# Recurrent attention followed by a squared-ReLU layer: the loads of the last twelve chunks move from SyncE's queue to GpSimd's

## The chip, the core and the metric

The kernel runs on one core of one Trainium2 chip, as a single launch. The metric is the time of one execution on the device in microseconds (us). The profile is one execution recorded by the hardware profiler; its times count from the first instruction of the program.

## What is computed

The first stage is a gated linear recurrence over 768 tokens, for 4 batches of 8 heads with 48 numbers each. The second is a layer with 2048 hidden units that works on the 3072 tokens and needs the eight heads of a token side by side:

```python
for t in range(S):
    state = alpha[:, :, t, :, None] * state + einsum('bhd,bhe->bhde', k[:, :, t], v[:, :, t])
    y[:, :, t] = einsum('bhd,bhde->bhe', q[:, :, t], state)
x = y.transpose(0, 2, 1, 3).reshape(B * S, H * D)     # 3072 x 384
h = x @ w_in                                          # 384 -> 2048
g = relu(h) ** 2
out = g @ w_out                                       # 2048 -> 384
```

All inputs and the output are float32 in HBM. In q, k, v and alpha the head stands ahead of the token, so one token of one head is a run of 48 numbers, 192 bytes.

## The kernel before

**Tiles.** The 3072 tokens are cut into 24 chunks of 128, six per batch, numbered 0 to 23 (`s` in the code). A chunk of q, k, v or alpha is loaded as one tile of 128 tokens by 8 heads by 48 numbers: 192 KB, that is 1024 runs of 192 bytes on the HBM side. Each of the four tile names (`qt`, `kt`, `vt`, `at`) has six buffers (`LB = 6`), so the tile of chunk s can be loaded once the user of chunk s-6 is through. Chunks 0 to 3 have their alpha loaded jointly; from chunk 10 on, the alpha of a chunk is loaded together with q, k and v of the chunk before it.

**One chunk of the recurrence.** ScalarE (ACT) takes the logarithm of alpha into `L_s` (L396). TensorE (PE) sums it along the tokens with a triangular matrix; ACT takes the exponential with both signs (L451, L454, L462, L466). q is multiplied by the decay and k by its inverse on VectorE (DVE). PE forms the scores `sc` (L555), DVE masks them into `sm` (L561), PE multiplies by v and adds the share of the running state (`py`, L592 and L601), ACT casts the result into `xn` (L610), and it is turned into `xT_big`, the input of the layer. The state is updated by PE, DVE and ACT (L572, L581, L586).

From chunk 11 on (`RAW = 11`) q and k are not turned by PE. GpSimd (POOL) casts the loaded tiles to bfloat16 (`rawb`, L413), and a DMA transpose on SyncE's (SP's) queue turns them (`rawt`, L416); DVE multiplies the turned tiles by the turned decay (L507, L510). v is cast by POOL in every chunk (`vb`, L405). For chunks 18 to 22 `xn` too is turned by a DMA transpose on SP (L620).

**The layer.** Groups of one, two or four token tiles run through w_in (L663), ReLU on ACT (L676), the square on DVE (L684), w_out (L732), an eviction (L756, L758) and a store. Ten of the stores, those of token tiles 8 to 17, are issued by POOL (L772), the others by SP.

**The order of the work.** The kernel writes its own schedule. Every piece of work is an `Op` with an engine, a planned duration, its dependences, a priority and a planned latency to its result (`lat`). `Plan.run` (L96) takes at each step the piece that can start first, smaller priority numbers ahead of larger ones, and fixes with that the order of the instructions of every engine. A gate lets a chunk of the recurrence start only 3.7 token tiles ahead of the layer's progress (L834 to L839). The loads on SP are a queue of their own in the plan, called DMA, taken strictly in the order in which they were added, each with 1.0 us of planned transfer (`LD1`) and 2.4 us to its landing. DMA transposes (`TR`) and stores by SP (`OUT`) are planned apart from it and occupy the same DMA time. A piece on another engine that has `moves` occupies DMA time as well. Planned dependences set the order alone; on the chip an instruction waits for the data and buffers that it needs and for the instructions ahead of it on its engine.

Of the kernel before, what the change touches and what calls it, by code (L numbers as in the profile page):

```python
# [54 lines left out]
def after(op, x=0.0):  # L55
    return (op, x)
# [85 lines left out]
def kernel(  # L142
# [10 lines left out]
    nc = tc.nc  # L153
# [40 lines left out]
        out=utri_f, in_=utri_f, compare_op=ALU.is_ge, fill=0.0,  # L194
# [10 lines left out]
    for c in range(JN):  # L205
        blk = slice(JP * c, JP * c + JP)
        nc.gpsimd.affine_select(
            out=tri4[blk, 0:JW], in_=tri4[blk, 0:JW], compare_op=ALU.is_ge, fill=0.0,
# [27 lines left out]
    def pin(ins):  # L236
        tc.keep_in_program_order(ins)
# [4 lines left out]
    def tr(*a):  # L242
        pin(nc.tensor.transpose(*a))  # L243
# [21 lines left out]
    def add(eng, dur, emit, *deps, **kw):  # L265
        return plan.add(Op(eng, dur, emit, deps, **kw))
# [41 lines left out]
    C = [dict() for _ in range(NT)]  # L308
    state = {}
    SRC = dict(srcs)  # L310
    EARLY = 4
    RAW = 11
    XTURN = (18, 23)
    TLD, TLAT, TLATE = 1.0, 4.0, 2.0
    NR = 3
# [48 lines left out]
    def add_load(s, nm):  # L364
        d = C[s]
        b, c = divmod(s, NCH)

        def ld():
            if nm not in d:
                d[nm] = loads.tile([P, H, D], FP32, name=nm)  # L370
            pin(nc.sync.dma_start(out=d[nm], in_=SRC[nm][b, c]))
        prev = C[s - LB].get("use_" + nm) if s >= LB else None
        d["ld_" + nm] = add("DMA", LD if s < 4 else LD1, ld, prev, lat=2.0 if s < 4 else LAG if s < 6 else 2.4, at=0.6)

    def add_chunk(s):
# [30 lines left out]

        raw = s >= RAW
        if raw:
            w, wz = s % NR, s % 2

            def e_rb(j, nm):
                raw_tiles()
                pin(nc.gpsimd.tensor_copy(R["b"][:, w, j, :, 0:D], d[nm]))  # L413

            def e_turn(j):
                pin(nc.sync.dma_start_transpose(out=R["t"][:, w, j], in_=R["b"][:, w, j].rearrange("p h d -> p (h d)")))  # L416
            rt = []
            for j, nm in enumerate(["qt", "kt"]):
                cb = add("POOL", 0.55, lambda j=j, nm=nm: e_rb(j, nm), d["ld_" + nm],
                         *([C[s - NR]["turn"][j]] if s >= RAW + NR else []), prio=-5.0)  # L420
                d["use_" + nm] = cb
                t_ = add("TR", TLD, lambda j=j: e_turn(j), cb, *([C[s - NR]["turned"][j]] if s >= RAW + NR else []), lat=TLAT)
                t_.late = TLATE
# [54 lines left out]
        if raw:  # L478
# [8 lines left out]
            aT = add("ACT", 0.48, e_AT, pT, after(ai) if ai else None, **g)  # L487
            aiT = add("ACT", 0.48, e_AiT, pT, after(aT), *([C[s - 2]["turned"][1]] if s >= RAW + 2 else []), **g)
            pT.gives = aiT
# [124 lines left out]
        def e_p4():  # L614
            d["px"] = psum(p4, [P, KT, P], BF16)
            for j in range(KT):
                tr(d["px"][:, j, :], d["xn"][:, j * P:(j + 1) * P], ident_bf)
        if XTURN[0] <= s < XTURN[1]:
            def e_xt():
                pin(nc.sync.dma_start_transpose(out=xT_big[:, :, s * P:(s + 1) * P], in_=d["xn"]))  # L620
# [164 lines left out]
    for d in DMA_ORDER + list(range(6, NT)):  # L785
        if d in ("i", "o"):
            load_w(d)
        elif d == "at":
            add_joint_alpha()
        elif isinstance(d, tuple):  # L790
            add_load(*d)
            if d[0] >= JN:
                if all("ld_" + nm in C[d[0]] for nm, _ in srcs):
                    add_chunk(d[0])
            elif d == JLAST:
                for s in range(JN):
                    add_chunk(s)
        else:
            for nm, _ in srcs:
                if nm != "at":  # L800
                    add_load(d, nm)
                elif d <= 9:
                    add_load(d, nm)
                if nm == "at" and 9 <= d < NT - 1:
                    add_load(d + 1, nm)
            add_chunk(d)
# [94 lines left out]
```

## Time and profile before

| what | value |
|---|---|
| median of 3 runs (lowest to highest) | 185.1 us (184.77 to 185.87) |
| the profiled execution's own time | 185.07 us |
| its span, first to last instruction | 183.4 us |
| TensorE clock granted | 1.00 throughout |
| PE / DVE / ACT / POOL busy in the span | 177.5 / 127.1 / 126.5 / 39.4 us |
| the four kinds of loads on SP, issue to landing, median | 3.6 to 4.0 us |
| ten stores on POOL, issue to landing, median | 3.1 us |

How to read it: an engine is busy while it executes; waits are not counted, nor is the issue of a DMA by SP. Of POOL, the busy time takes in the 5.5 us in which it issued its ten stores. One row of an issue shows how long it held its engine's sequencer, and another how long the data took to land. A "releaser" is what ended an engine's idle time. The DMA share is the mean busy share of the 16 DMA engines that serve all queues. In the rows of DMA queues, q1 is the hardware queue that SP feeds and q0 the software queue that POOL feeds.

### The profile page before, as it was taken

What the parts mean: (1) busy time and instruction counts of PE and PEld (TensorE: products, weight loads), DVE (VectorE), ACT (ScalarE), POOL (GpSimd) and SP (SyncE); (2) the same over time, 40 slices, a digit from 0 to 9 for tenths busy, and PEclk for the clock granted to TensorE, in tenths of its full rate; (3) what the DMA queues carried; (4) which work ended last, traced back from release to release, by engine and by line L of the source; (5) the groups of instructions that cost most, each with busy time, mean ns of one, the idle gap of its engine ahead of it and who ended that gap; (6) DMA issues with size and microseconds to landing.
All of it is one profiled execution on the core that took longest, in us unless ns stands there. A gap on an engine that the chain in (4) does not pass through costs nothing.

```text
span 183.4 us, 4946 instructions
## 1 busy us (share of the span) xinstructions
PE 177.5 (97%) x1908; PEld 130.5 (71%) x1908; DVE 127.1 (69%) x273; ACT 126.5 (69%) x286; POOL 39.4 (21%) x80
## 2 busy tenths in 40 slices
PE   7999999899999999999999998999999999999993
PEld 2577884567769877867768776667766777778663
DVE  1179898684999998778877867748855984744200
ACT  3677799226859996966967859847975895767321
POOL 8221100021131142132223133342323512000000
PEclk9999999999999999999999999999999999999999
DMA  5999999999999999998999599898898898901022
GB/s 168 215 212 252 302 366 321 326 220 204 177 191 201 194 179 173 141 190 161 150 193 202 113 240 186 161 227 162 170 201 182 176 163 194 301 13 43 12 77 86
DMA packets 120200, 34.12 MB, mean 186 GB/s; under 512 B 112400, under 2 KB 118928, under 8 KB 120176
## 3 DMA queue, kind: packets, MB, share of 16 engines
q1 hardware_dynamic: 119536, 31.83, 80.7%
q0 software_dynamic: 640, 1.97, 3.2%
q8 instruction: 15, 0.25, 0.6%
q14 instruction: 9, 0.07, 0.2%
HBM read 25.17 MB, written 4.72 MB: 163 GB/s over the span
## 4 chain that ended last, share of the span: by engine, by line
PE 49%; DMA 2%; ACT 1%; issue 0%; DVE 0%
PE bank L240 45%; DMA at<-in_alpha_dram 2%; PE sc L240 2%; PE st L240 1%; PE bank L243 1%; ACT aiT L454 0%; ACT r L676 0%; ACT ob L758 0%; ACT L_s L396 0%; ACT ob L716 0%; DVE xT_big L388 0%; ACT qkT L451 0%
## 5 line engine op out<-in xcount | busy, mean ns | idle before, releaser
L240 PE MATMUL bank<-xT_big,w_in_b 128*128 128x256 bf16 (+2 forms) x636 | 76.6, 262 | 0.9 <-ACT r L676 0.7
L240 PE MATMUL bank<-w_out_b,gT 128*128 128x384 bf16 (+1 forms) x400 | 71.6, 320 | 0.5 <-DVE w_out_b L296 0.5
L676 ACT ACTIVATE r<-bank 128x512 bf16<-128x512 f32 x96 | 56.6, 606 | 11.3 <-PE bank L240 9.9
L240 PEld LDWEIGHTS <-w_in_b 128*128 128x128 bf16 x636 | 52.7, 98 | 10.6 <-issue 1.5
L240 PEld LDWEIGHTS <-gT 128*128 128x128 bf16 x416 | 37.2, 98 | 18.7 <-DVE w_out_b L296 1.0
L684 DVE TENSOR_TENSOR gT<-r 128x512 bf16<-128x512 bf16 x96 | 41.8, 453 | 10.2 <-ACT r L676 9.0
L561 DVE TENSOR_TENSOR sm<-sc,utri_b 128x512 bf16<-128x512 f32 x48 | 30.8, 684 | 5.9 <-PE sc L240 5.7
L405 POOL CAST vb<-vt 128x384 bf16<-128x384 f32 x24 | 13.6, 569 | 69.1 <-DMA vt<-in_v_dram 55.2
L386 ACT CAST xn<-bank 128x384 bf16<-128x384 f32 x24 | 11.6, 482 | 11.6 <-PE bank L240 11.5
L505 DVE TENSOR_TENSOR kI_s<-kt,Ainv 128x384 bf16<-128x384 f32 x21 | 12.8, 611 | 7.8 <-ACT Ainv L466 7.8
L240 PEld LDWEIGHTS <-qkT 64*128 64x128 bf16 (+1 forms) x272 | 10.7, 95 | 6.4 <-issue 2.4
L586 ACT CAST sb<-st 128x384 bf16<-128x384 f32 x20 | 9.6, 482 | 7.7 <-DVE st L581 7.5
L758 ACT COPY ob<-bank 128x384 f32<-128x384 f32 x14 | 6.7, 480 | 8.0 <-PE bank L240 8.0
L396 ACT ACTIVATE L_s<-at 128x384 bf16<-128x384 f32 x20 | 10.5, 527 | 2.4 <-DMA at<-in_alpha_dram 2.3
L240 PE MATMUL bank<-warm 128*128 128x256 bf16 (+1 forms) x54 | 10.9, 348 | 1.3 <-DVE warm L188 1.3
L502 DVE TENSOR_TENSOR qA_s<-qt,A 128x384 bf16<-128x384 f32 x11 | 6.3, 575 | 8.0 <-ACT A L462 8.0
L413 POOL CAST rawb<-qt 128x384 bf16<-128x384 f32 x13 | 7.4, 570 | 20.3 <-DMA qt<-in_q_dram 20.3
L413 POOL CAST rawb<-kt 128x384 bf16<-128x384 f32 x13 | 7.6, 587 | 19.0 <-DMA kt<-in_k_dram 11.1
L581 DVE TENSOR_TENSOR st<-st,ae_s 128x384 f32<-128x384 f32 x20 | 11.1, 556 | 0.5 <-PE st L240 0.5
L466 ACT ACTIVATE Ainv<-bank 128x384 bf16<-128x384 f32 x21 | 10.5, 501 | 1.1 <-PE bank L240 1.0
L240 PE MATMUL sc<-qkT 64*128 64x128 bf16 x192 | 9.5, 219 | 0.0
L240 PEld LDWEIGHTS <-sm 128*128 128x128 bf16 x192 | 8.1, 96 | 1.7 <-issue 0.2
(64 smaller groups left out, 165.7 us busy)
## 6 DMA issues: line engine op xcount, KB each, us to landing
qt<-in_q_dram SPq DMA_DIRECT2D x24, 192.0 KB, 4.0
kt<-in_k_dram SPq DMA_DIRECT2D x24, 192.0 KB, 3.6
vt<-in_v_dram SPq DMA_DIRECT2D x24, 192.0 KB, 3.8
at<-in_alpha_dram SPq DMA_DIRECT2D x20, 192.0 KB, 4.0
wo<-in_moe_w_out_dram SPq DMA_DIRECT2D x4, 768.0 KB, 8.5
out_dram<-ob POOLq DMA_DIRECT2D x10, 192.0 KB, 3.1
wi<-in_moe_w_in_dram SPq DMA_DIRECT2D x4, 384.0 KB, 5.3
wi<-in_moe_w_in_dram SPq DMA_DIRECT2D x2, 768.0 KB, 8.3
```

What stands on the lines that cost most here:

```text
L240: pin(nc.tensor.matmul(*a, **kw))
L386: pin(nc.scalar.copy(out_t, in_t))
L396: pin(nc.scalar.activation(L[:, :, 0:D], d["at"], AF.Ln))
L405: pin(nc.gpsimd.tensor_copy(d["vb"], d["vt"]))
L413: pin(nc.gpsimd.tensor_copy(R["b"][:, w, j, :, 0:D], d[nm]))
L466: pin(nc.scalar.activation(d["Ai"], d["pm"][:, 0:HD].rearrange("p (h d) -> p h d", h=H), AF.Exp, scale=-1.0))
L505: pin(nc.vector.tensor_mul(kI[:, :, 0:D], d["kt"], d["Ai"]))
L561: pin(nc.vector.tensor_mul(d["sm"][:, hh], d["sc"][:, hh], utri_b.to_broadcast([P, NP, P])))
L581: pin(nc.vector.tensor_mul(st4, st4, bcast(ae, D)))
L586: pin(nc.scalar.copy(d["sbt"], d["st"]))
L676: pin(nc.scalar.activation(box["r"][:, 0:w], box["ph"][:, 0:w], AF.Relu))
L684: pin(nc.vector.tensor_mul(gT[g][:, f0:f0 + per, lo * P:lo * P + n], r, r))
```

## The change

Three constants are added, and a branch in `add_load`. For chunks 12 to 23 the tiles `at`, `qt`, `kt` and `vt`, 48 loads, are issued by POOL in place of SP. In the plan such a load takes 0.9 us of POOL, 0.85 us of DMA time and 5.0 us from the end of its issue to its landing; it may start once the scores (`p2`) of the chunk three before it are done, and its priority (4.0) stands behind that of the casts (-5.0) and ahead of that of POOL's stores (5.0). The size and the layout of each load, the buffers and everything that uses the tiles stay as they are. SP keeps its loads up to chunk 11, the weights, all DMA transposes and its stores. As the schedule is worked out anew, the order of the instructions can change on every engine.

```diff
@@ -310,6 +310,7 @@
     SRC = dict(srcs)
     EARLY = 4
     RAW = 11
+    PL, PL_AHEAD, PL_LAT = 12, 3, 5.0
     XTURN = (18, 23)
     TLD, TLAT, TLATE = 1.0, 4.0, 2.0
     NR = 3
@@ -368,8 +369,12 @@
         def ld():
             if nm not in d:
                 d[nm] = loads.tile([P, H, D], FP32, name=nm)
-            pin(nc.sync.dma_start(out=d[nm], in_=SRC[nm][b, c]))
+            pin((nc.gpsimd if s >= PL else nc.sync).dma_start(out=d[nm], in_=SRC[nm][b, c]))
         prev = C[s - LB].get("use_" + nm) if s >= LB else None
+        if s >= PL:
+            o = d["ld_" + nm] = add("POOL", 0.9, ld, prev, C[s - PL_AHEAD]["p2"], prio=4.0, lat=PL_LAT)
+            o.moves = 0.85
+            return
         d["ld_" + nm] = add("DMA", LD if s < 4 else LD1, ld, prev, lat=2.0 if s < 4 else LAG if s < 6 else 2.4, at=0.6)
 
     def add_chunk(s):
```

## The prediction

> **What bounds the kernel now.** I read the engines' totals first, then the table by stages, then the chain of work that ended last, then the rows of single operations that the change moves.
>
> ```profile
> PE 177.5 (97%) x1908; PEld 130.5 (71%) x1908; DVE 127.1 (69%) x273; ACT 126.5 (69%) x286; POOL 39.4 (21%) x80
> ```
> ```profile
> 60.00:80.00 20.00, 20.00 (x244) 16.19 (x241) 18.31 (x39) 16.60 (x39) 5.48 (x10) 1.00 0.96 174
> 80.00:100.00 20.00, 19.92 (x210) 14.79 (x209) 15.54 (x34) 14.98 (x35) 5.90 (x11) 1.00 1.00 176
> 100.00:120.00 20.00, 19.33 (x197) 14.24 (x196) 14.48 (x34) 15.84 (x37) 5.80 (x11) 1.00 0.90 180
> 120.00:140.00 20.00, 20.00 (x202) 14.09 (x199) 13.44 (x28) 14.52 (x35) 7.28 (x14) 1.00 0.91 189
> 140.00:160.00 20.00, 20.00 (x212) 15.18 (x211) 14.52 (x30) 14.75 (x34) 4.38 (x8) 1.00 0.88 200
> ```
>
> The columns are the stretch, its length, then PE, PEld, DVE, ACT and POOL busy, the clock, the DMA share and GB/s. The loads of chunks 12 to 23 lie between 60 and 150 us. There PE is idle for 0.08 + 0.67 = 0.75 us of 100. Its busy time is no stretched figure: in the chain below, 57 matmuls of the layer and the recurrence follow each other in 5.98 us, 105 ns apart. So PE's own work sets the time, and an earlier landing can give back 0.75 us at most. The chain has the one place where a load reached PE:
>
> ```profile
> 105.28 4.13 DMA at<-in_alpha_dram
> ...
> 109.42 0.34 ACT L_s L396
> ...
> 110.70 0.60 ACT aiT L454
> 111.30 0.49 ACT r L676
> 111.79 0.04 issue
> 111.84 0.49 PE bank L240 x3
> ...
> 146.09 5.98 PE bank L240 x57
> ```
>
> An alpha tile issued at 105.28 landed at 109.41. ACT, which works in order, stood at its logarithm; an eviction, two exponentials and a ReLU came late behind it, and PE waited 0.66 us for that ReLU. It is the whole loss of this stretch. After 162 us PE runs the rest of the layer, with no load left; before 60 us the loads are the same in both kernels.
>
> **The part taken from SP.** 48 of the 92 loads leave SP. While SP did little but load, 20 loads started from 39.98 to 60.76 us, 1.0 us apart, at a DMA share of 0.97. From 67 us on it has two transposes for each chunk besides. This frees SP and makes the transposes' issues earlier, by up to the load ahead of each, about 0.6 us; what they feed is hidden under PE's work, so I count 0. What is late next on SP is the POOL cast that a transpose needs.
>
> **The part put on POOL.** Each load's issue is a POOL instruction, in order with 36 casts and ten stores. The trace has POOL issuing stores alone, and SP issuing both kinds:
>
> ```profile
> L371 SPq DMA_DIRECT2D kt<-in_k_dram x24: 521/597/2482, 2.4 to 146.1; - x24
> L413 POOL CAST rawb<-kt x13: 507/508/804, 67.8 to 149.9; 128x384 bf16<-128x384 f32 x13
> ```
> ```profile
> L772 POOL DMA_DIRECT2D out_dram<-ob x10: 539/539/692, 97.1 to 152.9; - x10
> L772 SPq DMA_DIRECT2D out_dram<-ob x5: 332/332/350, 159.2 to 178.4; - x5
> ```
>
> The three numbers are least, median and most ns of one. A store is 192 KB in 128 runs of 1536 bytes, a load 192 KB in 1024 runs of 192 bytes. POOL's price for 1024 runs is the unknown of this change. One end: the number of runs does not matter, 0.54 us. The other: all of it grows with the runs, 8 x 0.54 = 4.3 us. The nearest row for the step from one form to the other is SP's: 332 ns becomes 521, a factor of 1.57. I take the same factor, 0.54 x 1.57 = **0.85 us**; it is an estimate, since another engine does the work. (The plan books 0.9.)
>
> Room on POOL: chunk 9's scores, after which chunk 12's loads may start, ran at 64.6 us; the last load on SP now starts at 146.7, so POOL should be through at about 148. In these 83.4 us POOL was busy for 26.6, stores included. That leaves 56.8 us for 48 issues, **1.18 us each**. At 0.85 they take 41 us, and POOL is 81% busy. So they fit, with 0.33 us to spare on each: cost on the path 0. Behind a burst of four issues (3.4 us) wait casts of q, k and v and the ten stores. The cover for that is the earlier start. Scores follow each other every 6.8 us (83.8 us for chunk 12, 158.6 for chunk 23, over 11), so three chunks are 20.4 us. Chunk 23's k is issued 12.5 us ahead of its scores now (146.1) and would be at about 20.4 - 3 x 0.85 = 18. For alpha it goes the other way: chunk 23's is issued 25.8 us ahead now (132.8), then about 20; its use is some 5 us ahead of the scores, which leaves 15 us. Each issue also waits for its buffer, last used by the chunk six before; that chunk is three chunks past when the issue comes, so I count no wait. If one waited, all casts would queue behind it.
>
> The Trainium skill has a rule on this price. The row: nine of ten POOL issues lie within 1 ns of 539, beside a DVE that is busy 13 to 18 of every 20 us, while casts go from 507 up to 804. The page "SBUF — State Buffer", section "Who interferes with whom", says that DVE instructions with two SBUF inputs shut out POOL instructions that read SBUF, and that DVE copies within SBUF in a two-port mode shut out even the writing of descriptors. By that rule, the trace agrees for the casts; whether a longer issue is hit more, no row here shows. By the row the sum stays; if the rule reached the issues too, it would be the waiting variant of rival (a).
>
> **DMA time.** A load on SP takes 1.0 us of all 16 engines (above). POOL's ten stores took 3.2% of 183.4 us for 1.97 MB, 0.59 us each:
>
> ```profile
> q1 hardware_dynamic: 119536, 31.83, 80.7%
> q0 software_dynamic: 640, 1.97, 3.2%
> ```
>
> The packet counts show why the two differ: q0 moved 3.1 KB per packet, q1 0.27 KB. A load on q0 lies between 0.59 (packed like the stores) and 1.0 us (no gain), or above if q0 reads short runs worse; nothing here excludes that, and twice SP's price is the bound I keep. I take 0.85. The four loads of a chunk then need 3.4 us in place of 4.0, at a share of 0.9 that is not the limit of PE: 0. At 2.0 us, four loads would need 8 us of every 6.8. Landing: the median is 3.1 us for POOL's stores, and 3.6 to 4.0 for loads on SP; the plan's 5.0 covers both.
>
> **The sum**, against the profiled execution (185.07 us, beside a median of 185.1): PE's work 0; the alpha wait gone, -0.66 at best; issues on POOL 0; a few new waits of a tenth of a us, as the order is planned anew, +0.2 to +0.5. That is -0.5 to +0.5; I take **184.9 us**.
>
> **Rivals.**
> (a) *POOL becomes the bound.* Above 1.18 us per issue every further 0.1 us costs 48 x 0.1 = 4.8 us, since casts, transposes, scores and then PE wait for POOL's order. At 1.5 us: 48 x 0.32 = +15, 200 us. At 4.3: +150, 335 us. For it: an eightfold number of runs, worked out by software, and the casts' stretching. Against it: SP's factor of 1.57. If each issue waited for one DVE instruction of 0.45 us (squares: 41.8 us for 96), 0.85 would become 1.30, and the time 191.
> (b) *Late landings reach PE.* Every engine works in order, so a load later than planned does again what the alpha did at 105 us, 0.66 us each time. Transposes and loads, now in two queues, contend for DMA engines that are 0.9 busy. One event in two chunks gives 6 x 0.66 = +4, 189 us. It decides once landings pass the planned 5.0 us; SP's alpha loads reached 8.8. Against it: 5 us more lead for k and v.
> (c) *More than 0.5% faster.* It needs 0.93 us, and the stretch holds 0.75. Only a new order of PE that also removes idle time elsewhere would do: 184.0.
> (d) *It does not load earlier.* The dependence on the scores stands in the plan alone, and alpha and q hardly move ahead. Then nothing changes: 185.1, within the forecast.
>
> **How the numbers follow.** Forecast with (d), within 0.5%: 0.50; (a) 0.24; (b) 0.18; (c) 0.08. A measurement of this kernel can tell about 0.5% (0.93 us) from no change. So faster 0.08, same 0.50, slower 0.42. The likeliest case's own range is 184.3 to 185.9. For 8 in 10 the range takes in (b) and (a) up to 1.5 us per issue; above that lies about 0.13, below 184.0 some 0.05: **184.0 to 200 us**.
>
> **What would show it.** POOL's issue row for the loads: 0.85 us right, over 1.18 wrong, and then POOL would be busy without gaps from 65 us on and PE would wait for the products with `rawt`. PE's idle time in 60 to 160 us: below 0.75 confirms the floor; several us, spread by chunk, with releasers at loads or turned tiles, is (b). q0's share: 48 loads at 0.85 us are 22% of the span; over 30% means that q0 reads short runs worse. The wait of ACT for alpha at 105 us should be gone. The forecast fails if the issue price is misjudged; that is its weakest step.

## The result and the profile after

| | before | after |
|---|---|---|
| median of 22 runs each (lowest to highest) | 185.06 us (183.6 to 188.54) | 186.52 us (184.66 to 188.41) |
| ratio after / before, 95% interval | | 1.0073 (1.0049 to 1.0097) |
| profiled execution: own time / span | 185.07 / 183.37 us | 186.2 / 184.05 us |
| the time outside the span | 1.70 us | 2.15 us |
| PE idle in 60 to 160 us | 0.75 us | 1.30 us |

The changed kernel is slower by 0.73%, about 1.4 us. The forecast was 184.9 us and no difference that can be told; the time lies in the range of 184.0 to 200, on the side that had the chance 0.42. Below, two profiled executions (of e9 and e12) took longer throughout than their kernels usually do, so only what lies behind their span and their fetches of instructions are read.

Lines of the code after `add_load` have moved down by 5: L421 is L416 of before, L625 is L620. First the engines' totals of the changed kernel:

```profile
PE 177.0 (96%) x1907; PEld 130.5 (71%) x1908; DVE 127.4 (69%) x274; ACT 126.2 (69%) x285; POOL 80.8 (44%) x128
```

POOL went from 39.4 to 80.8 us, the others stayed. The stages, with the columns of the prediction (stretch, length, PE, PEld, DVE, ACT, POOL, clock, DMA share, GB/s):

```profile
60.00:80.00 20.00, 19.87 (x242) 16.05 (x239) 18.10 (x40) 15.64 (x36) 14.19 (x20) 1.00 0.97 173
80.00:100.00 20.00, 19.99 (x213) 14.77 (x210) 15.03 (x32) 14.84 (x35) 16.50 (x24) 1.00 1.05 180
100.00:120.00 20.00, 19.76 (x202) 14.73 (x201) 16.63 (x36) 16.16 (x37) 15.39 (x23) 1.00 1.01 179
120.00:140.00 20.00, 20.00 (x204) 14.28 (x203) 13.41 (x28) 14.68 (x36) 17.11 (x25) 1.00 0.80 178
140.00:160.00 20.00, 19.08 (x201) 14.33 (x200) 12.96 (x27) 14.20 (x34) 6.25 (x11) 1.00 0.86 221
```

PE lost 0.24 us in 100 to 120, where it had lost 0.67, and 0.92 us in 140 to 160, where it had lost nothing. The chain that ended last shows what took the place of the alpha wait:

```profile
133.24 2.03 PE bank L240 x23
135.27 6.33 DMA xT_big<-xn
141.60 0.14 issue
141.74 4.17 PE bank L240 x36
```

PE's own sequence at that place, start and length first, shows the idle time in brackets:

```profile
140.46 0.36 PE L240 MATMUL bank<-vb,sm 128*128 128x48 bf16 x8
141.74 0.49 PE L240 MATMUL bank<-xT_big,w_in_b 128*128 128x256 bf16 x3 [0.92 <-DMA xT_big<-xn]
```

A transpose of `xn`, issued by SP at 135.27, landed at 141.60, 6.33 us later. The plan books 0.8 us for its issue and 4.0 us from there to its landing, 4.8 us in all. PE, in order, stood at the first product with that tile. No load was late: it is a transpose on SP's queue, which the change did not touch, that came late. How long the transfers took from issue to landing (kind, count, size, median us):

```profile
at<-in_alpha_dram POOLq DMA_DIRECT2D x12, 192.0 KB, 4.9
qt<-in_q_dram POOLq DMA_DIRECT2D x12, 192.0 KB, 5.1
kt<-in_k_dram POOLq DMA_DIRECT2D x12, 192.0 KB, 5.2
vt<-in_v_dram POOLq DMA_DIRECT2D x12, 192.0 KB, 4.6
...
rawt<-rawb SPq DMA_TRANSPOSE x26, 5.3
...
xT_big<-xn SPq DMA_TRANSPOSE x5, 3.3
```

Before, the same two rows of transposes stood at:

```profile
rawt<-rawb SPq DMA_TRANSPOSE x26, 3.4
...
xT_big<-xn SPq DMA_TRANSPOSE x5, 2.5
```

Last, the time outside the span. The DMA view of the 2.3 us behind the changed kernel's last instruction shows one packet; the same view of the kernel before shows none:

```profile
DMA packets 1, 0.01 MB, mean 4 GB/s; under 512 B 0, under 2 KB 0, under 8 KB 0
...
q14 instruction: 1, 0.01, 1.0%
```
```profile
DMA packets 0, 0.00 MB, mean 0 GB/s; under 512 B 0, under 2 KB 0, under 8 KB 0
```

It is a block of 8 KB of instructions, whose fetch begins 1.0 us after the last instruction of the span. The program's time is 0.45 us longer outside the span. This is not the mark of one execution: the changed kernel's 22 runs have 2.11 to 2.27 us outside the span, by the span that is listed for each, and all runs of the kernel before beside the experiments 1.66 to 1.84.

The accounting between the two profiled executions (+1.13 us) is then: +0.45 outside the span; +0.55 of PE's idle time in 60 to 160 us (1.30 against 0.75); +0.63 of idle time before 60 us, where both kernels load through SP alone; and -0.5 of PE's busy time (177.0 against 177.5). The last two are one execution against another: an unaltered second profile of the changed kernel (c1, below) has 5.3 us of idle time before 60 us where this one has 2.9.

### The profile page after: what moved, and what is told of

Same layout as the page of the kernel before. It is cut to its first block, busy times and chain, and to the rows that moved or that the text cites. A ratio compares the mean times of both kernels' runs of the same rounds, so it can differ in the third digit from the quotient of the medians.

```text
span 184.0 us, 4932 instructions
## 1 busy us (share of the span) xinstructions
PE 177.0 (96%) x1907; PEld 130.5 (71%) x1908; DVE 127.4 (69%) x274; ACT 126.2 (69%) x285; POOL 80.8 (44%) x128
## 4 chain that ended last, share of the span: by engine, by line
PE 70%; DMA 11%; DVE 9%; ACT 6%; issue 2%; SPq 0%; DVEq 0%; ACTq 0%
PE bank L240 62%; DMA wi<-in_moe_w_in_dram 5%; DVE gT L689 3%; DMA xT_big<-xn 3%; PE bank L243 3%; PE sc L240 3%; ACT r L681 2%; DMA at<-in_alpha_dram 2%; PE st L240 2%; DVE sm L566 1%; ACT A L467 1%; ACT Ainv L471 1%; DVE st L586 1%; DVE kI_s L510 1%; DVE w_out_b L296 1%
## 5 line engine op out<-in xcount | busy, mean ns | idle before, releaser
L240 PE MATMUL bank<-xT_big,w_in_b 128*128 128x256 bf16 (+2 forms) x635 | 75.5, 262 | 1.5 <-DMA xT_big<-xn 0.9
L689 DVE TENSOR_TENSOR gT<-r 128x512 bf16<-128x512 bf16 x96 | 42.8, 465 | 6.2 <-ACT r L681 5.3
L410 POOL CAST vb<-vt 128x384 bf16<-128x384 f32 x24 | 14.9, 622 | 53.9 <-DMA vt<-in_v_dram 49.2
L510 DVE TENSOR_TENSOR kI_s<-kt,Ainv 128x384 bf16<-128x384 f32 x21 | 12.2, 582 | 10.2 <-ACT Ainv L471 9.9
L240 PE MATMUL bank<-warm 128*128 128x256 bf16 (+1 forms) x54 | 10.0, 325 | 1.3 <-DVE warm L188 1.3
L372 POOL DMA_DIRECT2D at<-in_alpha_dram x12 | 10.8, 903 | 0.1
L372 POOL DMA_DIRECT2D qt<-in_q_dram x12 | 10.6, 885 | 0.0
L372 POOL DMA_DIRECT2D vt<-in_v_dram x12 | 10.6, 884 | 0.0
L372 POOL DMA_DIRECT2D kt<-in_k_dram x12 | 10.6, 883 | 0.0
```

Source lines behind the costliest of these rows:

```text
L240: pin(nc.tensor.matmul(*a, **kw))
L372: pin((nc.gpsimd if s >= PL else nc.sync).dma_start(out=d[nm], in_=SRC[nm][b, c]))
L410: pin(nc.gpsimd.tensor_copy(d["vb"], d["vt"]))
L510: pin(nc.vector.tensor_mul(kI[:, :, 0:D], d["kt"], d["Ai"]))
L689: pin(nc.vector.tensor_mul(gT[g][:, f0:f0 + per, lo * P:lo * P + n], r, r))
```

## The experiments

Three theories were at stake. **A, the queue:** POOL's loads make SP's transposes land later, and a late turned tile reaches PE. **B, the order:** the plan came out in another order, and that order costs something on whatever queue the loads are. **C, the code,** formed after the first four runs: the 0.45 us outside the span depend only on where POOL's program ends within a block of instructions. "Ratio" is against the kernel before, run on the same chip, with its 95% interval.

### e1: the new order, with all loads on SP

```diff
-            pin((nc.gpsimd if s >= PL else nc.sync).dma_start(out=d[nm], in_=SRC[nm][b, c]))
+            pin(nc.sync.dma_start(out=d[nm], in_=SRC[nm][b, c]))
```

> The changed kernel's plan and order of instructions, but the 48 loads are issued by SP in the places that the plan gives them. Theory A (what costs is the queue: turned tiles land late beside POOL's loads, and some 0.5 us that lie outside the span come with POOL's loads): the time outside the span goes back from 2.2 to 1.7 us, transposes land in about 3.4 us again, PE's wait for xT_big is gone, ratio to the kernel before 0.998 to 1.003. Theory B (the new order costs, whichever queue carries the loads): ratio 1.005 to 1.010 as in the change itself, with PE's wait for xT_big still there.

Measured: ratio 0.9998 (0.9956 to 1.0039). PE's idle time in 60 to 160 us is 0.24 us, and 1.71 us lie outside the span. `rawt` lands as early as before in the median, and the latest takes 4.8 us instead of 7.8 in the changed kernel; `xT_big` does not, 4.0 us against 2.5:

```profile
rawt<-rawb SPq DMA_TRANSPOSE x26, 3.4
...
xT_big<-xn SPq DMA_TRANSPOSE x5, 4.0
```

The median of five tiles tells little here; the tile that PE waited for, that of chunk 19, tells more. With the loads on SP it landed after 4.62 us, in time for PE; with the loads on POOL after 6.33, and after 5.86, 5.99 and 6.36 us in c1, e7 and e10 below; in e11, where SP loads again from chunk 18 on, after 3.57.

So the new order in itself costs nothing that can be measured, and the alpha wait goes in it too. What the changed kernel loses comes with the other queue or with what its use adds to the program.

### e2 and e3: no `xn` turned by DMA, with the loads on POOL and on SP

In both kernels:

```diff
-    XTURN = (18, 23)
+    XTURN = (18, 18)
```

> The changed kernel, but chunks 18 to 22 turn xn on PE as all other chunks do (XTURN empty), so that nothing of the layer's input passes a DMA transpose. PE gets 5 x 0.17 = 0.8 us more work. Theory A, if the late xT_big is the loss inside the span (0.9 us): it loses the 0.9 and pays 0.8, so the time is that of the change, ratio 1.005 to 1.009, and only about 0.5 us above the same edit on the kernel before (the run beside this one). Theory B: 1.35 us above that run, ratio 1.010 to 1.013.

> The kernel before with XTURN empty, as the partner of the run with the changed kernel. Both theories: 5 x 0.17 = 0.8 us more on PE and nothing else, ratio 1.003 to 1.006.

Measured: 1.0129 (1.0067 to 1.0191) with the loads on POOL, 1.0049 (1.0009 to 1.0088) on SP. The two are 0.8% apart. That is the number of theory B (1.010 to 1.013 and 1.35 us), not that of theory A (0.5 us), though the two intervals overlap; e1 speaks against B's reason, since there the same kind of new order cost nothing. PE's idle time in 60 to 160 us is 0.78 us on POOL and 0.00 on SP; `rawt` lands after 5.8 and 3.6 us. That suggests that `xT_big` is not the only tile through which the queue costs something. The time outside the span was 1.76 us in e2, though all 48 loads are on POOL: the 0.45 us are no price of POOL's loads. That led to theory C.

### e4: the loads on SP, and POOL's ten stores on SP too

```diff
-    POOL_OUT = (5, 18)
+    POOL_OUT = (5, 5)
```

> The kernel before with its ten stores on SP too, so that POOL issues no DMA at all. If the time outside the span grows with the number of DMAs issued by POOL (0.5 us for 48 loads, 0.01 each), it falls by only 0.1 us, from 1.7 to 1.6; if the first use of POOL's queue has a fixed price, it falls by more, and the 0.5 us of the change come from something else. The time itself: within 0.5% of the kernel before by theory A, as the stores are off the path; SP's queue gets 10 x 0.33 us more.

Measured: 1.0118 (1.0052 to 1.0184), a miss. 1.71 us lie outside the span, so POOL's stores have no part in that; but ten more issues on SP cost 1.2%. PE's waits in 60 to 160 us (us in total, times, longest):

```profile
PE bank L240 <- DMA xT_big<-xn: 1.3, 2, 1.0
PE sc L240 <- DVE qkT L510: 1.1, 1, 1.1
```

Both are turned tiles that came late, here because SP had no time to issue their transposes: `xT_big` landed 2.3 us after its issue in the median, but the first four of its five issues came 3.0 to 4.8 us after the tile was cast, where the kernel before has 2.3 to 3.1. In the kernel before, SP had little time to give away: added up from its trace, its issues fill 92% of 66 to 148 us, in the changed kernel 44%.

### e9: eight instructions on POOL that do nothing

```diff
     nc.gpsimd.memset(L4[:, :, :, D:], 0.0)
+    pad_t = consts.tile([P, 32], BF16)
+    for _ in range(8):
+        nc.gpsimd.memset(pad_t, 0.0)
```

> The changed kernel with eight small memsets more on POOL, issued before its first cast, where POOL idles. The changed kernel's trace has a fetch of 8 KB of instructions 1.0 us after the end of the span, and POOL has fetched after 69 recorded instructions and ends at 196, about 128 further on. Theory C (the 0.45 us outside the span are POOL's next block of instructions, asked for only at the program's end): with eight more instructions the fetch comes before the end, beside other work, and the time outside the span falls from 2.17 to 1.72 us, ratio to the kernel before 1.003 to 1.006. Rival (0.45 us is a price of POOL's loads as such, for their queue at the program's end): still 2.17 us, ratio 1.007.

Measured: 0.9997 (0.9954 to 1.0041). Outside the span lie 1.76 us, and the view of the stretch behind it has no packet:

```profile
DMA packets 0, 0.00 MB, mean 0 GB/s; under 512 B 0, under 2 KB 0, under 8 KB 0
```

The packet of 8 KB is now at 159.0 us, in the midst of the work. Eight more instructions took 0.39 us from the time outside the span, and in all 12 runs of e9 it lies between 1.67 and 1.81 us. The ratio came out below the forecast of 1.003 to 1.006, with an interval that takes in its lower end.

### e12: the kernel before, with 57 such instructions at the end of POOL's program

```diff
+    pad_t = consts.tile([P, 32], BF16)
...
+    for _ in range(57):
+        pin(nc.gpsimd.memset(pad_t, 0.0))
```

> The kernel before with 57 memsets of 32 numbers at the end of POOL's instructions, after its last store, where POOL only waits for the end: 139 + 57 = 196 recorded instructions, as many as in the changed kernel, and not one load moved. Theory C (POOL's next block of instructions is fetched at the program's end): the time outside the span rises from 1.72 to 2.17 us, the span stays, ratio 1.0025, with a fetch of 8 KB just after the span's end. Rival (the 0.45 us need loads issued by POOL): 1.72 us, ratio 1.000.

No load is moved here; POOL's program has only become as long as in the changed kernel (196 recorded instructions). Measured: 1.0024 (0.9975 to 1.0073), 2.19 us outside the span, and the packet is behind the span:

```profile
DMA packets 1, 0.01 MB, mean 3 GB/s; under 512 B 0, under 2 KB 0, under 8 KB 0
...
q14 instruction: 1, 0.01, 0.7%
```

With e9 this shows from both sides that the 0.45 us go with the length of POOL's program, and not with its loads: in all 12 runs of e12 2.12 to 2.21 us lie outside the span, in the 29 of the kernel before beside it 1.68 to 1.84. The ratios do not resolve it: 0.45 us are 0.24%, and each interval is wider. That a block is fetched behind the span is not enough, though: in e2 and e15 a fetch begins 0.6 us behind it, and only 1.76 and 1.78 us lie outside.

### e7 and e10: a realistic landing planned for the `xn` transposes

```diff
-            d["x"] = add("TR", 0.8, e_xt, xn, lat=TLAT)
+            d["x"] = add("TR", 0.8, e_xt, xn, lat=6.0)
```

e10 has the eight instructions of e9 as well.

> The changed kernel, but the plan books 6.0 us in place of 4.0 for the landing of the five turned xn, so that PE's order asks for them later. Theory A (inside the span the loss is PE's wait for a turned xn that landed 6.3 us after its issue): the wait of 0.9 us is gone, and nothing takes its place, ratio 1.001 to 1.004, with 2.1 to 2.2 us outside the span unless POOL's instruction count changes. Theory B (other small waits of the new order make the loss): ratio stays at 1.006 to 1.008, with waits at masks and turned tiles.

> Both edits at once, the eight memsets and the 6.0 us. Theories A and C together: both terms gone, ratio 0.998 to 1.001, and 1.72 us outside the span. If only one of the two holds, 1.002 to 1.005.

Measured: e7 1.0003 (0.997 to 1.0036), e10 1.0021 (0.998 to 1.0062). The wait for `xT_big` is gone in both, though the transposes land no earlier (4.4 us in the median). PE's idle time in 60 to 160 us is 0.74 and 0.56 us; e7 has 2.15 us outside the span, as theory C has it for an unpadded program, e10 1.84. e10 came out above its forecast of 0.998 to 1.001, which lies in its interval. That the two edits add up is not to be seen in the times.

### e11: POOL loads chunks 12 to 17 only

```diff
-            pin((nc.gpsimd if s >= PL else nc.sync).dma_start(out=d[nm], in_=SRC[nm][b, c]))
+            pin((nc.gpsimd if PL <= s < XTURN[0] else nc.sync).dma_start(out=d[nm], in_=SRC[nm][b, c]))
...
-        if s >= PL:
+        if PL <= s < XTURN[0]:
```

> POOL loads chunks 12 to 17 only; SP loads 18 to 23 again, as in the kernel before, so that no load is in POOL's queue while xn of chunks 18 to 22 is turned. Theory A (loads of the other queue delay the turned tiles): rawt of chunks 12 to 17 still lands late (5 us), xT_big lands in 2.5 us again and PE does not wait for it; POOL's instructions end away from a block's edge, so 1.72 us outside the span; ratio 0.998 to 1.002. Theory B: ratio 1.004 to 1.007, since most of the new order is kept.

Measured: 1.0013 (0.9978 to 1.0049), with no wait for `xT_big`. Its use is that one execution holds both queues. From 66 to 104 us POOL has most of the loads (21, beside 7 of SP), and the DMA view says:

```profile
q0 software_dynamic: 1338, 4.11, 55.5%
...
rawt<-rawb SPq DMA_TRANSPOSE x11, 6.1
```

From 110 to 150 us all loads are SP's:

```profile
q0 software_dynamic: 482, 1.45, 16.2%
...
rawt<-rawb SPq DMA_TRANSPOSE x11, 3.4
```

The same transposes, eleven in each stretch, land after 6.1 us beside POOL's loads and after 3.4 us beside SP's. The engines were somewhat busier in the first stretch too (q0 and q1 together 109% of their time, by the sum of the packets' times, against 94%); how much of the 2.7 us is due to that, e11 does not tell. The kernel before and the changed one tell something in 110 to 150 us, where q0 and q1 together take 88% of the engines' time in both: `rawt` lands there after 3.4 us in the one and 4.4 in the other. With e1 this shows the first half of theory A: `rawt` lands later where POOL loads. By what means is not shown.

### c1: the changed kernel once more, unaltered

> The changed kernel once more, unaltered, as a control beside the two others of this call. Expected again: ratio 1.005 to 1.010 and 2.17 us outside the span. If it comes out at 1.002 to 1.004, the share inside the span is smaller than the first measurement had it, and the time outside the span is most of what can be told apart.

Measured: 1.0036 (0.9995 to 1.0078), 2.15 us outside the span, and the wait at the same place of the chain, now 0.4 us long:

```profile
134.98 2.04 PE bank L240 x23
137.02 5.86 DMA xT_big<-xn
```

PE's idle time in 60 to 160 us is 0.70 us against 1.30 in the first profile. So the two marks, the late tile and the packet at the end, come back each time, and the size of the first varies.

### e13: the alpha wait of the kernel before mended in the plan

```diff
-        d["ld_" + nm] = add("DMA", LD if s < 4 else LD1, ld, prev, lat=2.0 if s < 4 else LAG if s < 6 else 2.4, at=0.6)
+        d["ld_" + nm] = add("DMA", LD if s < 4 else LD1, ld, prev, lat=2.0 if s < 4 else LAG if s < 6 else 4.2 if nm == "at" else 2.4, at=0.6)
```

> The kernel before with 4.2 us in place of 2.4 planned for the landing of the alpha loads from chunk 6 on, so that ACT's order asks for the logarithm when the tile is there. If the wait at 105 us is what an earlier alpha could give back (0.66 us), PE has no wait between 60 and 160 us, ratio 0.995 to 0.998. If other waits take its place, 0.999 to 1.004.

Measured: 1.0142 (1.0101 to 1.0182), a miss. The wait of 0.66 us is gone, a wait of 1.0 us behind an exponential (`ae_s`) came at about 62 us, and the time rose by 1.4%. A new order can cost more than the wait for which it was made; one wait taken off is no forecast of a time.

### e14 to e17: eleven `xn` turned by SP instead of five

Both kernels with chunks 12 to 22 turned by DMA, which takes 18 of 57 matmuls of `xn` off PE; without and with the planned landing of 6.0 us:

```diff
-    XTURN = (18, 23)
+    XTURN = (12, 23)
```

e14 is that edit in the kernel before, e15 in the changed one. e17 is e14 with the edit of e7, and e16 is e15 with those of e7 and e9.

> The kernel before, with xn turned by SP from chunk 12 on (eleven chunks in place of five). PE saves 6 x 0.17 = 1.0 us. Theory A: the turned xn share a queue with the loads and land in about 2.5 us, so no new wait, ratio 0.994 to 0.998, unless SP, which has four loads and two transposes for each chunk already, issues them late.

> The changed kernel, with xn turned by SP from chunk 12 on. PE saves the same 1.0 us. Theory A: the turned xn meet POOL's loads eleven times, land in 3 to 6 us against 4.0 planned, and PE waits for two or three of them, 1.5 to 3 us in all; ratio 1.005 to 1.015, and at least 1.5 us above the partner with loads on SP. Theory B (the order as such): PE's waits for xT_big do not grow, ratio 1.000 to 1.004.

> The same, with 6.0 us planned for the landing of the turned xn and the eight memsets on POOL that move its instruction block. Theory A: PE's waits for xT_big are gone, PE keeps the 1.0 us that it saves, ratio 0.994 to 0.999, which would be the fastest of the kernels with loads on POOL. Theory B: as in the run before this one, less 0.45 us at most.

> The kernel before with xn turned by SP from chunk 12 on and 6.0 us planned for its landing, as the partner of the run above with loads on SP. Both theories: 0.994 to 0.999; if SP is too full for eleven more transposes, waits for turned tiles appear and it comes out above 1.000, and the run with loads on POOL beats it.

| | loads on SP | loads on POOL |
|---|---|---|
| eleven `xn` turned by SP | e14: 1.0309 (1.0227 to 1.0391) | e15: 0.998 (0.994 to 1.002) |
| the same, landing of 6.0 us planned | e17: 1.0274 (1.0206 to 1.0342) | e16: **0.9865** (0.981 to 0.992) |
| PE idle in 60 to 160 us | 2.88 and 4.46 us | 0.81 and 0.00 us |

For e15 theory A wanted 1.005 to 1.015, as more tiles can be late: a miss. The waits for `xT_big` came to 0.2 us only. e14 (0.994 to 0.998 forecast) missed as well, and e16 gained more than its forecast of 0.994 to 0.999; e17 came out as its second case had it. On SP the same edit costs about 3%, and SP's own sequence in e17 suggests why (start, length, instruction):

```profile
118.83 1.20 SPq L416 DMA_TRANSPOSE rawt<-rawb  x1
120.08 0.58 SPq L371 DMA_DIRECT2D qt<-in_q_dram  x1
120.77 1.20 SPq L416 DMA_TRANSPOSE rawt<-rawb  x1
122.01 0.58 SPq L371 DMA_DIRECT2D kt<-in_k_dram  x1
122.64 0.58 SPq L371 DMA_DIRECT2D vt<-in_v_dram  x1
123.26 0.79 SPq L371 DMA_DIRECT2D at<-in_alpha_dram  x1
124.15 1.88 SPq L620 DMA_TRANSPOSE xT_big<-xn  x1
126.14 1.20 SPq L416 DMA_TRANSPOSE rawt<-rawb  x1
```

Each instruction begins within 0.11 us of the end of the one before. SP is full with its issues, and the chain of e17 runs through three of these issues and the landing of the v load after them:

```profile
120.08 0.58 SPq L371
...
120.77 1.20 SPq L416
...
122.01 0.58 SPq L371
...
122.64 3.75 DMA vt<-in_v_dram
```

With the loads on POOL these issues are gone from SP, and the plan with the longer landing keeps PE busy without a gap. How much of the distance between e16 and e17 is the order's, and not the queue's, was not tried: e16's order with its loads on SP is missing. The stage of 60 to 160 us in e16, then in e17:

```profile
60.00:160.00 100.00, 100.00 (x1073) 76.11 (x1068) 78.26 (x160) 78.66 (x182) 70.71 (x99) 1.00 0.99 192
```
```profile
60.00:160.00 100.00, 95.54 (x1014) 71.06 (x1012) 72.52 (x153) 73.48 (x172) 26.99 (x50) 1.00 0.99 181
```

e16 is the fastest kernel of the study, faster than both. Its profiled execution beats that of the changed kernel by 186.2 - 182.54 = 3.66 us: 1.9 of PE's busy time (177.0 to 175.1; the 18 matmuls are an estimated 1.0 of it, at 0.17 us for three, and the rest is not explained), 1.3 of PE's idle time over the whole span (7.0 to 5.7) and 0.44 outside the span.

## Why the prediction was wrong, point by point

**PE bounds the kernel, with 0.75 us to gain:** right. Nothing in the result asks for another bound; e16 gains 2.5 us on the profiled execution of before, and PE's busy time falls by 2.4 (177.5 to 175.1).

**POOL's issue price, 0.85 us, and its room:** right. The least, median and most ns of a k load and of a store on POOL:

```profile
L372 POOL DMA_DIRECT2D kt<-in_k_dram x12: 882/882/891, 69.2 to 140.0; - x12
```
```profile
L777 POOL DMA_DIRECT2D out_dram<-ob x10: 540/569/572, 96.3 to 153.6; - x10
```

0.88 us, 1.55 times the median store of this kernel and 1.64 times the 0.54 of the kernel before, where SP's factor of 1.57 had been taken. Some luck is in this: the factor came from SP's least issue of a load, 521 ns, and its median of 597 would have made it 1.80 and the price 0.97 us. In 64.6 to 148 us POOL was busy for 66.73 of 83.4 us, 80%, where 81% had been worked out. Rival (a) is out: PE's waits name no cast by POOL. Nor did the waiting variant come true: these twelve issues lie within 9 ns of each other. (In the prediction's row of stores it is eight of ten that lie at 539 ns; a ninth took 542.) By the rule of the Trainium skill ("SBUF — State Buffer", "Who interferes with whom") DVE copies within SBUF in a two-port mode would hold up the issues; between 66 and 142 us DVE's copies all read the matmul banks, so no run here tests that.

**DMA time of a load, 0.85 us:** too low, and without effect. The shares of the queues in the changed kernel:

```profile
q1 hardware_dynamic: 69616, 22.39, 53.3%
q0 software_dynamic: 3712, 11.41, 30.8%
```

q0 took 0.308 x 184.05 = 56.7 us, 5.9 of them for ten stores at 0.59; the rest over 48 loads is 1.06 us, against 1.0 on SP. All 48 take 27.6% of the span, where 22% had been worked out. q0 packs 16 runs into a packet (3072 packets for 48 loads, 3 KB each) and gains nothing by it.

**Landing within the planned 5.0 us:** right in the median (4.6 to 5.2 us from the start of the issue, where the plan has 0.9 and 5.0). No wait of PE or ACT names a load by POOL. Chunk 23's k was issued at 140.0, 18 us ahead of its scores at 158.0, as worked out. Its alpha was issued 20 us ahead, as worked out too, but its use was misread: the logarithm ran 11.8 us ahead of the scores and not 5, which left 8.3 us and not 15. That was enough.

**The alpha wait goes:** right. **Few new waits, +0.2 to +0.5 us:** this is the first step that failed. What the transposes feed was counted as "hidden under PE's work, so I count 0", with only the gain of an earlier issue in view, about 0.6 us. That gain was larger: SP issued the first four turned `xn` 2.3 to 3.1 us after their cast had ended in the kernel before, and at once (0.02 to 0.03 us) in the changed one. But the landing of the transposes went from 3.4 to 5.3 us for `rawt` and up to 6.3 for `xT_big`. Counted from the cast, four of the five `xT_big` still landed earlier than before; that of chunk 19 took 6.35 us instead of 5.10, PE asked for it 5.6 us after the cast, and so it reached PE (0.92 us, 0.4 in c1), with a wait of 0.24 us for a mask beside it. Late landings were named in rival (b), with contention of the two queues as the reason, which stays open; one came instead of six. In one execution it more than ate the 0.66 us of the alpha wait (idle 0.75 to 1.30), in the other it just balanced it (0.70).

**Time outside the span, unchanged:** this is the other step that failed. The sum was made against the profiled execution's own time, with what lies around the span taken as fixed. It rose by 0.45 us, as POOL's program had grown to a length at which another block of instructions is fetched behind the span (e9 and e12). It belongs to no rival.

**What stays open.** 0.45 us are a third of the loss of 1.4 us. The waits that the traces show inside the span explain between nothing and 0.6 us more. The rest is not settled. By the spans of all runs the kernel lost 0.65 us inside the span beside c1 (median 184.75 us against 184.1) and e9, with the same order and eight idle instructions, 0.05 (184.25 against 184.2); c1 puts the whole loss at 0.36% with an interval that holds both zero and the first value, and the variants that mend one of the two marks (e7, e9, e10, e11) all lie within 0.3% of the kernel before, too close to each other to be ranked.

## What to carry to other kernels

Price a queue's neighbours too: a transfer that stays where it was can land later once another queue's loads run beside it, so its planned landing must be measured anew; e7 lost its wait by nothing else, though no gain in time can be told from that. A move of issues off a full sequencer can pay when something useful is put in the room that it makes: the move alone gave 1.0073, and with six more transposes on SP, the landing planned anew and the eight idle instructions 0.9865, where the old queue gave 1.0274. Look at the time outside the span when a program grows: a block of instructions that is fetched 1 us behind the last one cost 0.45 us here and went away with a few instructions more.

## What the runs showed of the hardware

- Beside POOL's loads, in packets of 3 KB, SP's transposes took 6.1 us to land, beside SP's own loads 3.4 (e11). The Trainium skill ("DMA: Bandwidth & Descriptors", "Issuing engines are not separate DMA queues") says that transfers of all engines interleave on the same DMA engines, and that issuing from several saves only the sequencer's time, usually a small thing. The trace agrees with the first (q0 and q1 took 55.5% and 53.7% of the time of the same engines). Here the sequencer's time seems no small thing: SP's issues fill 92% of 66 to 148 us in e17 and 54% in e16, and the two are 4% apart, the order's part in it untried.
- POOL's issue price differs with the form of the transfer, but less than the number of runs: for 192 KB 0.57 us with 128 runs (a store), 0.88 us with 1024 (a load).
- The instructions on queue q14 come in blocks of 8 KB. Where the fetch of a block began 1.0 to 1.2 us behind the span, the time outside was 2.15 to 2.19 us (after, c1, e7, e12); where it began up to 0.6 us behind it (e2, e11, e15) or within the span, 1.70 to 1.84 us. That the block is POOL's is inferred from e9 and e12; for e11 it is not known.
